# A gated mix of a state-space layer and a GELU MLP: the recurrence as VectorE prefix scans over 256 tokens, GELU as one table function, the first x transposed by TensorE

## The chip, the cores and the metric

The kernel runs on one core of a Trainium2 chip. The metric is the time of one execution on the device in microseconds (us), lower is better. Names of engines as in the profile: PE is TensorE (PEld its weight loads), DVE is VectorE, ACT is ScalarE, POOL is GpSimd, SP is the engine that issues most DMAs.

## What is computed

x has 2048 tokens of 640 features. The state h has 640 complex entries per token; the MLP has 1728 hidden units. All weights are bf16.

```python
g = sigmoid((x * gate_w).sum(-1, keepdims=True))
# a: state-space layer
Lam_bar = exp(dt * Lam)                         # dt = exp(log_dt), Lam complex
Bu = einsum("bld,pd->blp", x, ((Lam_bar - 1.0) / Lam)[:, None] * Bmat)
for t in range(L):
    h = Lam_bar[None, :] * h + Bu[:, t, :]
a = 2.0 * einsum("blp,dp->bld", hseq, Cmat).real + x * Dskip
# b: MLP
b = gelu(x @ w1 + b1) @ w2 + b2                 # tanh form of gelu
out = g * a + (1 - g) * b
```

## The kernel before

**Data.** xT holds x with features on partitions, loaded by transposing DMAs (L334 for the first 512 tokens, L343 for the rest); W1sb, W2sb, BT and CT hold the weights. SP issues all large loads in one fixed order: first half of w1, first x, rest of w1, rest of x, B, w2, C; then, chunk by chunk, x again with tokens on partitions (xtk, L904) and the outputs (L934).

**MLP, in four quarters q of 512 tokens** (`make_mlp`). For each of 14 slices of 128 hidden units (the last has 64) PE runs five 128x512 matmuls into one of two PSUM banks (L651) and ACT copies the bank out with the bias (Ub, L660). Over four slices at a time GELU is computed as u*sigmoid(c*u*(1+0.044715u²)): three DVE passes (L672, L675, L678), a sigmoid on ACT (L686) and a fourth DVE pass into Gl (L693). m2 (L882) then multiplies Gl by W2, 14 matmuls of 128x320 for each half of the output columns.

**State-space layer, in 16 chunks c of 128 tokens** (`make_chunk`). bp (L730) multiplies x by B with tokens on partitions, the gate column beside it; ACT copies it out (L739). DVE multiplies by a complex table that undoes the decay (pre, L763 to L767). PE then sums over the tokens of the chunk by a triangular matrix (L789) and adds the carried state (L791). ACT copies the sums out (L801), DVE computes the next carry (L813 to L817) and multiplies by the complex table of the decay (post, L826 to L830). cp (L852) multiplies by C. ACT scales both branches by the gate (L862, L891) and DVE adds them up (L912, L921, L924).

**Order.** `Sched` is a list scheduler over planned durations; each engine gets its items in one fixed order, the state-space chain at higher priority than the MLP. An engine waits at the head of its queue for semaphores; all items behind it wait too.

Of the kernel before, what the change touches and what calls it, by code (L numbers as in the profile page):

```python
# [13 lines left out]

# [133 lines left out]

def bass_gated_mix__ssm_conv_s5__dense_activation_gelu__prompt_kernel(
# [39 lines left out]
    x2 = A_x[0]

    GC = math.sqrt(0.044715)
    GK = 2.0 * math.sqrt(2.0 / math.pi)
    TWO_PI = 2.0 * math.pi

    with ExitStack() as es, nc.Block() as block:
# [5 lines left out]
        xtk = [SB(f"xtk_{i}", [128, D], BF16) for i in range(2)]  # L201
        xDc = [SB(f"xDc_{i}", [128, D], BF16) for i in range(2)]
        W1sb = SB("W1sb", [128, KD, F], BF16)
        W2sb = SB("W2sb", [128, NF, D], BF16)
        XG = 2
        PADB = 16
        assert (P + PADB) * 2 % 32 == 0 and XG <= PADB
        BT = SB("BT", [128, KD, 2, P + PADB], BF16)
        CT = SB("CT", [128, KP, 2, D], BF16)
        dsk_bc = SB("dsk_bc", [128, D], BF16)  # L210
        b1col = SB("b1col", [128, NF], FP32)
        rows5 = SB("rows5", [KP, 4, 128], BF16)
# [3 lines left out]
        dtf = SB("dtf", [128, KP], FP32)  # L216
        acol = SB("acol", [128, KP], FP32)
        thcol = SB("thcol", [128, KP], FP32)
        io_i = SB("io_i", [128, T + 1], I32)
        io_f = SB("io_f", [128, T + 1], FP32)  # L220
        sg_i = SB("sg_i", [128, T + 1], I32)
        sg_f = SB("sg_f", [128, T + 1], FP32)
        ident = SB("ident", [128, 128], BF16)
        utri = SB("utri", [128, 128], BF16)
        NTB = T + 1
        es_wk = ExitStack()
        es_wk.__enter__()
        WK = [es_wk.enter_context(nc.sbuf_tensor(f"wk{i}", [128, KP, NTB], FP32)) for i in range(7)]
        kq_i = es_wk.enter_context(nc.sbuf_tensor("kq_i", [128, KP, NTB], I32))
        es_wk.__exit__(None, None, None)  # L230
        NES = 6
        Essm = [SB(f"Essm_{i}", [128, D], BF16) for i in range(NES)]
        assert NES * D * 2 <= 8 * KP * NTB * 4
        _pad_wk = SB("pad_wk", [128, (8 * KP * NTB * 4 - NES * D * 2) // 2], BF16)
        ang, tmp1, psi, kq_f, s2t, s4t, magp = WK
        magn = WK[0]
        sint = WK[2]
        cost = WK[3]
        chf = kq_i[:, :, :].bitcast(FP32)
        lr_t, li_t = WK[1], WK[4]  # L240
        nr_t, ni_t = WK[5], WK[6]
        mtmp = [WK[0], WK[2]]
        cwk = SB("cwk", [128, 8, KP], FP32)
        mr_t = SB("mr_t", [128, KP, T], BF16)
        mi_t = SB("mi_t", [128, KP, T], BF16)
        TA = SB("TA", [128, KP, 2, T], BF16)
        TB1 = SB("TB1", [128, KP, 1, T], BF16)
        TBp = TB1[:, :, :, :].broadcast_to([128, KP, 2, T])
        TTa = SB("TTa", [128, KP, 2], BF16)
        TTb = SB("TTb", [128, KP, 2], BF16)  # L250
        MA1 = SB("MA1", [128, 1, P], BF16)
        MA = MA1[:, :, :].broadcast_to([128, 2, P])
        MBp = SB("MBp", [128, 2, P], BF16)
        NU2 = 2
        U2 = [SB(f"U2_{i}", [128, 2, P], BF16) for i in range(NU2)]
        Wt = SB("Wt", [128, 2, P], BF16)
        NUT = 2
        Ut = [SB(f"Ut_{i}", [128, 2, P], BF16) for i in range(NUT)]
        NS2 = 2
        S2 = [SB(f"S2_{i}", [128, KP, 2, T], BF16) for i in range(NS2)]  # L260
        W2t = SB("W2t", [128, KP, 2, T], BF16)
        NH = 2
        Hb = [SB(f"Hb_{i}", [128, KP, 2, T], BF16) for i in range(NH)]
        Rb = SB("Rb", [128, NCH + 1, KP, 2], BF16)
        Rv = SB("Rv", [128, KP, 2], FP32)
        Rw = SB("Rw", [128, KP, 2], FP32)
        gcol = SB("gcol", [128, NCH], FP32)
        g1col = SB("g1col", [128, NCH], FP32)
        NE = 2
        Emlp = [SB(f"Emlp_{i}", [128, D], BF16) for i in range(NE)]  # L270
        osb = [SB(f"osb_{i}", [128, D], BF16) for i in range(2)]
        GROUPS = []
        j = 0
        while j < NF - 1:
            GROUPS.append(list(range(j, min(j + 4, NF - 1))))
            j += 4
        GROUPS.append([NF - 1])
        NGS = 3
        Ub = [SB(f"Ub_{i}", [128, 4, 512], BF16) for i in range(NGS)]
        Qb = [SB(f"Qb_{i}", [128, 4, 512], BF16) for i in range(NGS)]  # L280
        Ib = Qb
        Sgb = Qb
        Gl = [SB(f"Gl_{i}", [128, NF, 512], BF16) for i in range(2)]

        PSB = [es.enter_context(nc.psum_tensor(f"psb{i}", [128, 512], FP32)) for i in range(8)]
        BK_MLP1 = [0, 1]
        BK_ACC = [2, 3]
        BK_U = [4, 5]
        BK_G = [6, 7]

        semnames = [
            "ld_w1a", "ld_w1b", "ld_B", "ld_w2", "ld_C", "ld_misc", "ld_xt0", "ld_xt1", "outdma0", "outdma1",
            "ld_xq0", "ld_xq1",
            "pool", "ld_rows",
            "pe_mlp1", "pe_acc", "pe_u", "pe_g", "pe_misc",
            "act_u", "act_g", "act_e", "act_gate", "act_U", "act_sq", "act_sg", "act_misc",
            "dve_ut", "dve_h", "dve_r", "dve_in", "dve_gl", "dve_o", "dve_misc", "dve_misc2",
        ]
        sems = {n: es.enter_context(nc.semaphore(n)) for n in semnames}
        engines = {"sp": nc.sync, "act": nc.scalar, "dve": nc.vector, "pe": nc.tensor, "pool": nc.gpsimd}  # L300
        E = Emitter(nc, engines, sems)
        sch = Sched()

        def d_act(n):
            return 0.28 + n * 0.00085

        def d_dve(n, mode=1):
            return 0.17 + n * 0.00105 / mode

        def d_mm(n):  # L310
            return max(0.06, n / 2300.0)

        def d_dma(nbytes):
            return 2.0 + nbytes / 150e3

        FH = (NF // 2) * 128

        def f_ld_w1a(eg):
            ins = nc.sync.dma_start(W1sb[:, :, 0:FH], B_w1[:, 0:FH].rearrange("(k p) f -> p k f", p=128))
            return E.inc("sp", ins, "ld_w1a", 16)  # L320

        it_ld_w1a = sch.add("ld_w1a", "sp", 1.0, [], f_ld_w1a, prio=-10, lat=4.0)

        def f_ld_w1b(eg):
            ins = nc.sync.dma_start(W1sb[:, :, FH:F], B_w1[:, FH:F].rearrange("(k p) f -> p k f", p=128))
            return E.inc("sp", ins, "ld_w1b", 16)

        it_ld_w1b = sch.add("ld_w1b", "sp", 1.0, [], f_ld_w1b, prio=-8.9, lat=4.0)
        it_ld_w1 = [it_ld_w1a, it_ld_w1b]

        def f_ld_xq0(eg):
            t = None
            for k in range(KD):
                ins = nc.sync.dma_start_transpose(xT[:, k, 0:512], x2[0:512, k * 128:(k + 1) * 128])  # L334
                t = E.inc("sp", ins, "ld_xq0", 16)
            return t

        it_ld_xq0 = sch.add("ld_xq0", "sp", 1.4 * KD, [], f_ld_xq0, prio=-9, lat=3.0)

        def f_ld_xq1(eg):  # L340
            t = None
            for k in range(KD):
                ins = nc.sync.dma_start_transpose(xT[:, k, 512:S], x2[512:S, k * 128:(k + 1) * 128])  # L343
                t = E.inc("sp", ins, "ld_xq1", 16)
            return t

        it_ld_xq1 = sch.add("ld_xrest", "sp", 2.2 * KD, [], f_ld_xq1, prio=-8.5, lat=6.0)
        it_ld_xq = [it_ld_xq0] + [it_ld_xq1] * (NQ - 1)

        def f_ld_small(eg):  # L350
            E.wait("sp", it_w2pad.done)
            nc.sync.dma_start(W2sb[64:65, NF - 1, :], B_b2.rearrange("(o n) -> o n", o=1)).then_inc(sems["ld_misc"], 16)
            E.count["ld_misc"] += 16
            E.producer.setdefault("ld_misc", "sp")
            ins = nc.sync.dma_start(dsk_bc[:, :], A_Dskip.partition_broadcast(128))
            return E.inc("sp", ins, "ld_misc", 16)

        it_ld_small = sch.add("ld_small", "sp", 1.6, [], f_ld_small, prio=-8, lat=2.0)

        def f_ld_B(eg):  # L360
            t = None
            for k in range(KD):
                for ci, src_ in enumerate((A_B_re, A_B_im)):
                    ins = nc.sync.dma_start_transpose(BT[:, k, ci, 0:P], src_[:, k * 128:(k + 1) * 128])
                    t = E.inc("sp", ins, "ld_B", 16)
            return t

        it_ld_B = sch.add("ld_B", "sp", 1.32 * 2 * KD, [], f_ld_B, prio=-7, lat=6.0)

        def f_ld_w2(eg):  # L370
# [250 lines left out]
        def mark(key, it_):  # L621
            last_use[key] = [it_]
# [391 lines left out]
```

## Time and profile before

| what | value |
|---|---|
| three timed runs | 266.10, 265.36, 266.09 us (median 266.09) |
| span of the profiled execution | 262.7 us |
| median less span | 3.4 us |
| instructions | 4561 |

The span runs from the first to the last instruction of the profiled execution; the time of a run has a few us around it. A group line of the profile reads: line, engine, operation, output<-inputs, shapes, count | busy us, mean ns of one | idle time of the engine just before, and what ended most of it. Matmuls are pipelined, so the mean of one is longer than the step from one to the next; the step is read from a run of many. The other lines are quoted in the prediction where they are used.

### The profile page before, as it was taken

Reading aid. Unit: us, or ns where it says so; the run is one execution under the profiler, and the core shown is the slowest. Engines: PE = TensorE matmul, PEld = TensorE weight load, DVE = VectorE, ACT = ScalarE, POOL = GpSimd, SP = SyncE. Lnnn points to the kernel's source line nnn. Section 1 sums busy time; section 2 is a strip of 40 time slices with the busy share of each in tenths; the row PEclk is TensorE's granted clock in tenths of the full one; section 3 lists DMA queues with packets and bytes.
Section 4 is the critical chain, followed back from the end, with each engine's and each line's share of the span. In section 5 each row is a group of like instructions: output and inputs, shape, how many; then the busy total and the mean of one; then the engine's idle time right before and its main releaser. Section 6 shows DMA issues by size and latency. Waiting matters only on the chain.

```text
span 262.7 us, 4561 instructions
## 1 busy us (share of the span) xinstructions
PE 234.3 (89%) x1863; PEld 161.4 (61%) x1863; DVE 192.5 (73%) x370; ACT 151.1 (58%) x287; POOL 4.0 (2%) x13
## 2 busy tenths in 40 slices
PE   0597608999999999999999999999999998699994
PEld 0232205757767868888889875646777543477773
DVE  3454999687998998869796966897967348972432
ACT  1179906866868747545527626686734277653231
POOL 6000000000000000000000000000000000000000
PEclk9999977999999999999999999999999999999999
DMA  7999689730000000010100010100021100021211
GB/s 214 240 204 179 125 229 260 132 72 25 2 0 0 2 0 2 26 52 2 50 2 1 11 41 2 50 0 2 25 76 52 50 0 2 0 75 51 76 50 50
DMA packets 32037, 16.02 MB, mean 61 GB/s; under 512 B 24785, under 2 KB 32018, under 8 KB 32018
## 3 DMA queue, kind: packets, MB, share of 16 engines
q1 hardware_dynamic: 31826, 15.74, 24.5%
q8 instruction: 14, 0.23, 0.4%
q0 software_dynamic: 192, 0.01, 0.1%
q14 instruction: 5, 0.04, 0.1%
HBM read 7.22 MB, written 2.62 MB: 37 GB/s over the span
## 4 chain that ended last, share of the span: by engine, by line
PE 79%; DVE 9%; ACT 7%; SPq 2%; DMA 1%; issue 1%; DVEq 0%; ACTq 0%
PE psb L882 23%; PE psb L651 17%; PE psb L852 17%; PE psb L730 16%; PE psb L789 3%; PE psb L791 3%; ACT Ub L660 3%; SPq L334 2%; ACT Qb L686 2%; DVE Qb L672 1%; DVE Qb L678 1%; DMA xT<-in_A_x_dram 1%; DVE Qb L675 1%; ACT L484 0%; DVE Gl L693 0%
## 5 line engine op out<-in xcount | busy, mean ns | idle before, releaser
L651 PE MATMUL psb<-xT,W1sb 128*128 128x512 bf16 (+1 forms) x280 | 67.9, 396 | 12.8 <-ACT Ub L660 12.4
L882 PE MATMUL psb<-W2sb,Gl 128*128 128x320 bf16 x448 | 63.2, 299 | 2.2 <-ACT Ub L660 2.2
L651 PEld LDWEIGHTS psb<-xT,W1sb 128*128 128x128 bf16 (+1 forms) x280 | 27.3, 102 | 48.3 <-issue 13.1
L882 PEld LDWEIGHTS psb<-W2sb,Gl 128*128 128x128 bf16 x448 | 43.2, 98 | 20.0 <-ACT Ub L660 3.0
L660 ACT ACTIVATE Ub<-psb,b1col 128x512 bf16<-128x512 f32 (+1 forms) x56 | 37.4, 684 | 25.7 <-PE psb L651 18.8
L730 PE MATMUL psb<-BT,xT 128*128 128x256 bf16 (+2 forms) x480 | 49.4, 255 | 0.1
L852 PE MATMUL psb<-CT,Hb 128*128 128x320 bf16 x320 | 45.8, 299 | 0.0
L730 PEld LDWEIGHTS psb<-BT,xT 128*128 128x128 bf16 x480 | 40.1, 98 | 4.6 <-ACT U_0 L739 0.3
L852 PEld LDWEIGHTS psb<-CT,Hb 128*128 128x128 bf16 x320 | 31.3, 98 | 12.2
L891 ACT ACTIVATE Emlp<-psb,g1col 128x320 bf16<-128x320 f32 x32 | 16.8, 526 | 32.8 <-PE psb L882 32.8
L686 ACT ACTIVATE Qb<-Qb 128x2048 bf16<-128x2048 bf16 (+2 forms) x20 | 27.8, 1397 | 2.3 <-DVE Qb L678 2.2
L672 DVE TENSOR_TENSOR Qb<-Ub 128x2048 bf16<-128x2048 bf16 (+2 forms) x20 | 18.0, 898 | 12.2 <-ACT Ub L660 12.1
L862 ACT ACTIVATE Essm<-psb,gcol 128x320 bf16<-128x320 f32 x32 | 16.1, 528 | 12.6 <-PE psb L852 11.4
L789 PE MATMUL psb<-utri,Ut 128*128 128x128 bf16 x160 | 21.3, 219 | 0.5 <-DVE Ut L767 0.5
L791 PE MATMUL psb<-Rb,ident 128*128 128x128 bf16 x160 | 21.3, 219 | 0.0
L924 DVE TENSOR_TENSOR osb<-osb,Emlp 128x640 bf16<-128x640 bf16 x16 | 7.9, 492 | 17.7 <-ACT Emlp L891 17.4
L693 DVE TENSOR_TENSOR Gl<-Ub,Qb 128x2048 bf16<-128x2048 bf16 (+2 forms) x20 | 17.6, 896 | 3.6 <-ACT Qb L686 3.6
L678 DVE TENSOR_TENSOR Qb<-Qb,Ub 128x2048 bf16<-128x2048 bf16 (+2 forms) x20 | 18.1, 904 | 0.7
L739 ACT CAST U_1<-psb 128x512 bf16<-128x512 f32 (+1 forms) x24 | 12.2, 521 | 10.1 <-PE psb L730 10.1
L789 PEld LDWEIGHTS psb<-utri,Ut 128*128 128x128 bf16 x160 | 15.6, 98 | 1.9 <-DVE Ut L767 0.8
L739 ACT CAST U_0<-psb 128x512 bf16<-128x512 f32 (+1 forms) x24 | 12.3, 516 | 7.3 <-PE psb L730 7.3
L791 PEld LDWEIGHTS psb<-Rb,ident 128*128 128x128 bf16 x160 | 15.7, 98 | 1.1
(113 smaller groups left out, 196.1 us busy)
## 6 DMA issues: line engine op xcount, KB each, us to landing
xtk<-in_A_x_dram SPq DMA_DIRECT2D x16, 160.0 KB, 2.2
out_dram<-osb SPq DMA_DIRECT2D x16, 160.0 KB, 1.8
W2sb<-in_B_w_dram SPq DMA_DIRECT2D x1, 2080.0 KB, 8.6
W1sb<-in_B_w_dram SPq DMA_DIRECT2D x1, 1120.0 KB, 6.0
W1sb<-in_B_w_dram SPq DMA_DIRECT2D x1, 1040.0 KB, 6.0
xT<-in_A_x_dram SPq DMA_TRANSPOSE x10, 5.1
dsk_bc<-in_A_Dskip_dram SPq DMA_DIRECT2D x1, 160.0 KB
BT<-in_A_B_re_dram SPq DMA_TRANSPOSE x5, 3.7
```

Of the source, the lines that this page charges most:

```text
L651: ins = nc.tensor.matmul(PSB[bank][0:rows, :], W1sb[:, k, jf * 128:jf * 128 + rows], xT[:, k, q * 512:(q + 1) * 512], start=(k == 0), stop ...
L660: ins = nc.scalar.activation(Ub[slot][0:rows, jj, :], PSB[bank][0:rows, :], ACT.Identity, bias=b1col[0:rows, jf:jf + 1])
L672: t = E.inc("dve", nc.vector.tensor_tensor(out=Qb[slot][0:rows, 0:ng, :], in0=Ub[slot][0:rows, 0:ng, :], in1=Ub[slot][0:rows, 0:ng, :], op ...
L678: ins = nc.vector.tensor_tensor(out=Ib[slot][0:rows, 0:ng, :], in0=Qb[slot][0:rows, 0:ng, :], in1=Ub[slot][0:rows, 0:ng, :], op=ALU.mult)
L686: ins = nc.scalar.activation(Sgb[slot][0:rows, 0:ng, :], Ib[slot][0:rows, 0:ng, :], ACT.Sigmoid, scale=GK)
L693: ins = nc.vector.tensor_tensor(out=Gl[gsl][0:rows, grp[0]:grp[0] + ng, :], in0=Ub[slot][0:rows, 0:ng, :], in1=Sgb[slot][0:rows, 0:ng, :], ...
L730: t = nc.tensor.matmul(PSB[bank][:, o0:o0 + n_], xT[:, k, c * T:(c + 1) * T], BT[:, k, ci, pb0:pb0 + n_], start=(k == 0), stop=(k == KD - 1))
L739: ins = nc.scalar.copy(U2[u2s][:, :, pb0:pb0 + pw], PSB[bank][:, 0:2 * (pw + xg)].rearrange("p (a w) -> p a w", a=2)[:, :, 0:pw])
L789: nc.tensor.matmul(PSB[bank][:, col0:col0 + T], Ut[uts][:, ci, k * 128:(k + 1) * 128], utri[:, :], start=True, stop=False)
L791: t = nc.tensor.matmul(PSB[bank][:, col0:col0 + T], ident[:, :], Rb[:, c, k, ci:ci + 1].broadcast_to([128, T]), start=False, stop=True)
L852: t = nc.tensor.matmul(PSB[bank][:, 0:HALF], Hb[hs][:, k, ci, :], CT[:, k, ci, hf * HALF:(hf + 1) * HALF], start=(i == 0), stop=(i == 2 * ...
L882: t = nc.tensor.matmul(PSB[bank][:, 0:HALF], Gl[gsl][:, jf, tq * T:(tq + 1) * T], W2sb[:, jf, cols], start=(jf == 0), stop=(jf == NF - 1))
```

## The change

The kernel is written anew around the same mathematics; the two matrix products of the MLP and the product with C keep their shapes.

- **x.** The first 512 tokens arrive with tokens on partitions (`xn`) and PE transposes them in 20 steps (`tp`); DVE and ACT copy them to xT in turn (`tpe`). The other tokens still come by transposing DMA. xn also serves for the gate and the skip term, so the loads of xtk are gone; xn of later quarters is loaded by SP after C. w1 comes in three pieces. The small vectors come through ACT's DMA queue.
- **GELU.** One ACT instruction reads the PSUM bank and writes Gl. The four DVE passes and the sigmoid are gone. m1 has four PSUM banks, shared with the product by B.
- **State-space layer.** The product with B puts the state on partitions (B is the weight, 512 tokens move). For each block of 256 tokens DVE multiplies by a unit rotation (`pre`), runs two real prefix scans h = a*h + v, real and imaginary part (`scan`), rotates the carry, and rotates back (`post`). The sums and the carry on PE, the copies after them, and the chunk tables are gone. The rotation tables are outer products of 16 by 16 angles. A scan covers five state groups of 256 tokens in one instruction; the decay is set to 0 at the start of each group.
- **Gate and output.** The gate sums are DVE instructions with an accumulator (`gates`), its sigmoid is 0.5+0.5*tanh. Two additions on DVE form the output (`cmb`), a third instruction the skip term (`xg`).

```diff
-                            ins = nc.tensor.matmul(PSB[bank][0:rows, :], W1sb[:, k, jf * 128:jf * 128 + rows],
-                        ins = nc.scalar.activation(Ub[slot][0:rows, jj, :], PSB[bank][0:rows, :], ACT.Identity,
-                ins = nc.scalar.activation(Sgb[slot][0:rows, 0:ng, :], Ib[slot][0:rows, 0:ng, :], ACT.Sigmoid, scale=GK)
...
+                    return inc("act", nc.scalar.activation(Gl[q % 2][0:n, jf, :], PS[bank][0:n, :], ACT.Gelu_apprx_tanh, bias=b1col[0:n, jf:jf + 1]))
...
+                    t = nc.tensor.transpose(ps[:, k * 128:(k + 1) * 128], xn[0][:, c, k * 128:(k + 1) * 128], ident[:, :])
...
+            t = inc("dve", nc.vector.tensor_copy(out=atab[:, :, :], in_=amag[:, :].unsqueeze(2).broadcast_to([128, KP, T])))
+            E.wait("dve", t)
+            return inc("dve", nc.vector.memset(atab[:, :, 0:1], 0.0))
...
+        def gates(q):
+                    t = inc("dve", nc.vector.scalar_tensor_tensor(out=scr[:, :], in0=xn[q % 2][:, c, :], scalar=1.0, in1=gwb[:, :],
+                                                                  op0=ALU.mult, op1=ALU.mult, accum_out=gz[:, q * 4 + c:q * 4 + c + 1]))
...
+                            t = nc.tensor.matmul(PS[bank][:, :], BT[:, kd, ci, k * 128:(k + 1) * 128], xT[:, kd, q * 512:(q + 1) * 512],
...
+            def f_pre():
+                t1 = tt(v, bc(mr), u, ALU.mult)
+                t2 = tt(w, bc(mi), u, ALU.mult)
+                E.wait("dve", t1, t2)
+                tt(v[:, 0, :], v[:, 0, :], w[:, 1, :], ALU.add)
+                return tt(v[:, 1, :], v[:, 1, :], w[:, 0, :], ALU.subtract)
...
+                    t = tt(V[:, :, :, 0], V[:, :, :, 0], cz[:, :, :], ALU.add)
+                for ci in range(2):
+                    t = inc("dve", nc.vector.tensor_tensor_scan(out=g[:, ci, :], data0=a, data1=v[:, ci, :], initial=0.0, op0=ALU.mult, op1=ALU.add))
+                if b < NB - 1:
+                    tt(cz[:, :, :], rb(0), ge, ALU.mult)
+                    t = tt(cy[:, 0:2, :], rb(1), ge, ALU.mult)
+                    tt(cz[:, 0, :], cz[:, 0, :], cy[:, 1, :], ALU.add)
+                    t = tt(cz[:, 1, :], cz[:, 1, :], cy[:, 0, :], ALU.subtract)
...
+            def f_cmb():
+                t = tt(osb[c % NO][:, :], xg[c % 2][:, :], E1[c % NE][:, :], ALU.add)
+                E.wait("dve", t)
+                return tt(osb[c % NO][:, :], osb[c % NO][:, :], E2[c % NE][:, :], ALU.add)
...
+        gates(0)
+        m1(0)
+        m1(1)
+        bproj(0)
...
+        for q in range(2, NQ):
+            m1(q)
+            bproj(q)
+            ssm(2 * q)
+            xnload(q, prio=500 * q)
+            gates(q)
+            outs(q - 1)
+            ssm(2 * q + 1)
+        outs(NQ - 1)
```

The orders below list instructions as each engine has them in its queue. First PE at the start of the program, before (rows and b1rows are small vectors, L651 is the first product of the MLP):

```order
L979 UNCONDITIONAL_BRANCH
L439 MATMUL psb<-ident,rows 128x5 x4
L440 MATMUL psb<-ident,b1rows 128x14
L651 MATMUL psb<-xT,W1sb 128x512 x10
L979 UNCONDITIONAL_BRANCH
L651 MATMUL psb<-xT,W1sb 128x512 x10
```

PE at the same place now (xn is x with tokens on partitions, L597 the first product of the MLP):

```order
L808 UNCONDITIONAL_BRANCH
L394 MATMUL ps<-ident,xn 128x128 x5
L415 MATMUL ps<-ident,rows 128x5 x3
L416 MATMUL ps<-ident,b1rows 128x14
L394 MATMUL ps<-ident,xn 128x128 x15
L808 UNCONDITIONAL_BRANCH
L597 MATMUL ps<-xT,W1sb 128x512 x20
```

The transposes of x now stand ahead of the first product, and those of the small vectors among them.

PE in the middle, where the first outputs are made. Before, one chunk's items mix with the next one's (L882 m2, L852 cp, L789 and L791 the sums, L730 bp):

```order
L882 MATMUL psb<-W2sb,Gl 128x320 x14
L979 UNCONDITIONAL_BRANCH
L852 MATMUL psb<-CT,Hb 128x320 x20
L789 MATMUL psb<-utri,Ut 128x128
L791 MATMUL psb<-Rb,ident 128x128
```

PE there now (L618 the product with B of the second quarter, L693 m2, L717 the product with C):

```order
L618 MATMUL ps<-xT,BT 128x512 x20
L693 MATMUL ps<-W2sb,Gl 128x320 x28
L808 UNCONDITIONAL_BRANCH
L693 MATMUL ps<-W2sb,Gl 128x320 x14
L717 MATMUL ps<-CT,H 128x320 x20
L693 MATMUL ps<-W2sb,Gl 128x320 x14
L808 UNCONDITIONAL_BRANCH
L717 MATMUL ps<-CT,H 128x320 x20
L693 MATMUL ps<-W2sb,Gl 128x320 x28
L808 UNCONDITIONAL_BRANCH
L693 MATMUL ps<-W2sb,Gl 128x320 x28
L597 MATMUL ps<-xT,W1sb 128x512 x15
```

The sums are gone from PE, and three halves of m2 stand between the product with B and the first product with C, which needs H of the first block of 256 tokens.

DVE for one chunk of 128 tokens before (carry, post, and pre of a later chunk):

```order
L813 TENSOR_TENSOR Rv<-TTa,S_0 128x10
L814 TENSOR_TENSOR Rw<-TTb,S_0 128x10
L816 TENSOR_TENSOR Rb<-Rv,Rw 128x5
L817 TENSOR_TENSOR Rb<-Rv,Rw 128x5
L826 TENSOR_TENSOR Hb<-TA,S_0 128x1280
L827 TENSOR_TENSOR W2t<-TB,S_0 128x1280
L829 TENSOR_TENSOR Hb<-Hb,W2t 128x5x128
L830 TENSOR_TENSOR Hb<-Hb,W2t 128x5x128
L763 TENSOR_TENSOR Ut<-MA,U_1 128x1280
L764 TENSOR_TENSOR Wt<-MBp,U_1 128x1280
L766 TENSOR_TENSOR Ut<-Ut,Wt 128x640
L767 TENSOR_TENSOR Ut<-Ut,Wt 128x640
```

DVE for one block of 256 tokens now (pre, scan at L658, carry, post; L467 is the line of a helper, c and s are the tables of post):

```order
L467 TENSOR_TENSOR V<-mr,U 128x2560
L467 TENSOR_TENSOR W<-mi,U 128x2560
L467 TENSOR_TENSOR V<-V,W 128x1280 x2
L658 SCALAR_TENSOR_TENSOR G<-atab,V 128x1280 x2
L467 TENSOR_TENSOR cz<-rho,G 128x10
L467 TENSOR_TENSOR cy<-rho,G 128x10
L467 TENSOR_TENSOR cz<-cz,cy 128x5 x2
L467 TENSOR_TENSOR H<-c,G 128x2560
L467 TENSOR_TENSOR W<-s,G 128x2560
L467 TENSOR_TENSOR H<-H,W 128x1280 x2
```

The whole recurrence of a block is now one run on DVE without a step on PE or ACT; the scans stand between pre and post. The tables of functions on ACT are loaded three times in both programs (L457, L484, L686 before; at the first exponential, the first sine and the first GELU now).

More of the change, by code (lines that the diff above doesn't have):

```diff
@@ L261, in bass_gated_mix__ssm_conv_s5__dense_activation_gelu__prompt_kernel @@
[L261 to L266, printed above, removed]
+        amag = SB("amag", [128, KP], FP32)
+        io_i = SB("io_i", [128, 128], I32)
+        io_f = SB("io_f", [128, 128], FP32)
+        st_i = SB("st_i", [128, NS], I32)
+        st_f = SB("st_f", [128, NS], FP32)
+        ident = SB("ident", [128, 128], BF16)
@@ L267, in bass_gated_mix__ssm_conv_s5__dense_activation_gelu__prompt_kernel @@
         gcol = SB("gcol", [128, NCH], FP32)
         g1col = SB("g1col", [128, NCH], FP32)
+        scr = SB("scr", [128, D], BF16)
         NE = 2
[L270 to L279, printed above, removed]
@@ L937, in make_chunk @@
[L937 to L949 removed]
+                    return inc("pe", t)
+                op(f"c_{c}_{hf}", "pe", 2 * KP * d_mm(HALF), [("H", b % NHB), "CT"], [("bank", bank)], f_mm, prio=pe_prio())
@@ new lines, in outs @@
+        def outs(q):
+            for c in range(4 * q, 4 * q + 4):
+                m2(c)
+                cproj(c)
+                comb(c)
+        gates(0)
+        m1(0)
+        m1(1)
+        bproj(0)
+        ssm(0)
+        ssm(1)
+        xnload(1, prio=500)
+        gates(1)
+        bproj(1)
+        ssm(2)
+        outs(0)
+        ssm(3)
+        for q in range(2, NQ):
[6 more added lines that the diff above has]
+            ssm(2 * q + 1)
```

984 lines of the change are left out of this document (389 added, 595 removed).

## The prediction, made before the changed kernel ran

> **What bounds the kernel now.** I read the busy times, the busy slices, the chain and the waits of PE, in this order.
>
> ```profile
> span 262.7 us, 4561 instructions
> PE 234.3 (89%) x1863; PEld 161.4 (61%) x1863; DVE 192.5 (73%) x370; ACT 151.1 (58%) x287; POOL 4.0 (2%) x13
> PE   0597608999999999999999999999999998699994
> DVE  3454999687998998869796966897967348972432
> PE 79%; DVE 9%; ACT 7%; SPq 2%; DMA 1%; issue 1%; DVEq 0%; ACTq 0%
> 66.00:140.00 74.00, 74.00 (x727) 59.38 (x726) 63.91 (x131) 46.79 (x104) 0.00 (x0) 1.00 0.04 13
> PE psb L651 <- ACT Ub L660: 12.4, 6, 7.0
> ```
>
> PE holds 79% of the chain, and from 66 to 140 us it is busy all 74 us, at a granted clock of 1.00. There nothing but fewer or cheaper matmuls gains time. It is idle in the first 10 us, partly so until 44 us (slices of 6.6 us), and at two places near the end. The largest wait of PE, 12.4 us, is for ACT's copies Ub, which in turn wait for the GELU chain on ACT and DVE. DVE is next in line with 192.5 us.
>
> How long PE's work takes without waits I read from long runs in the chain and, for the sums, from the distance of two rows with 16 sums between them (start, us, what):
>
> ```profile
> 9.96 7.17 PE psb L651 x20
> 71.74 1.66 PE psb L730 x20
> 169.53 4.32 PE psb L651 x20
> 190.26 5.43 PE psb L852 x40
> 236.47 22.83 PE psb L882 x168
> ...
> 70.68 0.22 PE L789 MATMUL psb<-utri,Ut 128*128 128x128 bf16 x1
> 71.58 1.82 PE L730 MATMUL psb<-BT,xT 128*128 128x130 bf16 x20
> ```
>
> A step is 4.32/20 = 0.216 us with 512 columns, 22.83/168 = 0.136 with 320 (L852 the same), and 0.90/16 = 0.056 for a sum. So the kernel before holds 280 x 0.216 + 768 x 0.136 + 16 x 2.74 (L730: 1.66 and 1.09 per chunk) + 320 x 0.056 = 60.5 + 104.3 + 43.8 + 17.9 = 226.5 us of PE work; the other 36 us of the span are the start, waits and the tail. The first 20 matmuls took 7.17 instead of 4.32 us: a slow start of 2.85 us.
>
> **What PE does after the change.** The sums go (-17.9). The product with B becomes 200 matmuls of 512 columns, 43.2 us (-0.6). MLP and C stay. PE's work from the first product on is 60.5 + 43.2 + 104.3 = **208.0 us**. If PE never waits, the span is start + slow start + 208 + tail. So three questions are left: when PE starts, whether ACT and DVE keep up, and the tail.
>
> **The start.** Rows of the DMA issues (KB each, us from issue to landing), the column chain, DVE and the tail:
>
> ```profile
> xtk<-in_A_x_dram SPq DMA_DIRECT2D x16, 160.0 KB, 2.2
> W1sb<-in_B_w_dram SPq DMA_DIRECT2D x1, 1040.0 KB, 6.0
> rows<-in_A_Lambda_re_dram POOLq DMA_DIRECT2D x1, 1.2 KB, 5.3
> ...
> 0.74 0.45 SPq L319 DMA_DIRECT2D W1sb<-in_B_w_dram  x1
> 9.33 0.27 PE L439 MATMUL psb<-ident,rows 5*128 5x5 bf16 x4 [9.33 <-DMA b1rows<-in_B_b_dram]
> 10.96 0.83 DVE L469 TENSOR_TENSOR wk<-thcol,sg_f 128x645 f32<-128x645 f32 x1
> ...
> L548 DVE TENSOR_TENSOR wk<-wk,cwk 128x640 f32<-128x640 f32 x1 | 0.8, 827 | 0.0
> L472 DVE TENSOR_SCALAR wk<-wk 128x645 f32<-128x645 f32 x1 | 0.5, 499 | 0.0
> L593 DVE COPY MA<-psb 128x640 bf16<-128x640 bf16 x1 | 0.5, 483 | 0.0
> ```
>
> xn has 640 KB; between 2.2 us at 160 and 6.0 at 1040 KB that is 4.3 us, so it lands at 0.74 + 4.3 = 5.0. Twenty transposes at twice a sum's step (the slow start's ratio or a little more), 2.2 us, and the columns end at about 7.8. But the third copy into xT stands on DVE behind the angle chain: columns at 5.9, plus 1.6 (9.33 to 10.96 before) is 7.5, five operations of 165 elements with their waits 1.6, the decay table of 1280 f32 elements 0.8 to 1.5 (the rates of L472 and L548), the copy 0.5: 10.5 to 11.1. The small loads on ACT's queue have no row: bounds are 2.2 us (SP) and 5.3 us (POOL). The latter puts the columns 2 us later, so the first product starts at 10.5 to 13.1. I take **11.5**, near the SP row since ACT's queue issues like SP's (one more stretch than that, because these loads share the engines with xn). Before it was 9.96: the change loses 1.5 here. The slow start I keep at 2.85; bounds nothing, if the transposes already end it, and 2.85.
>
> The Trainium skill, "TensorE: Matmul & The Clock Gate", Part 1, has the array at half clock until about 3.4 us of activity; the trace's 20 matmuls lost 2.85, which fits a longer stretch of some 5.7 us. By the page's figure the loss is an estimated 1.7 and the sum 1 us less.
>
> **Does ACT keep up?** Rows by form:
>
> ```profile
> L660 ACT ACTIVATE Ub<-psb,b1col 128x512 bf16<-128x512 f32 x52 | 34.7, 684 | 23.5 <-PE psb L651 17.1 <-DVE Gl L693 6.3
> L686 ACT ACTIVATE Qb<-Qb 128x512 bf16<-128x512 bf16 x4 | 2.6, 638 | 0.0
> L891 ACT ACTIVATE Emlp<-psb,g1col 128x320 bf16<-128x320 f32 x32 | 16.8, 526 | 32.8 <-PE psb L882 32.8
> ```
>
> A copy with bias takes 0.68 us, and a table function (sigmoid) of the same size 0.64: no dearer. GELU has no row; between these two it fits into the 5 x 0.216 = 1.08 us in which PE fills the next of four banks, and would up to 1.08. So the 12.4 us of waits go, and ACT is not late next. In the output stage it has four copies of 0.53 in 6.5 us. No table is loaded in the loops, as the change's section says.
>
> **Does DVE keep up?** This is what is late next.
>
> ```profile
> L672 DVE TENSOR_TENSOR Qb<-Ub 128x2048 bf16<-128x2048 bf16 x12 | 14.6, 1221 | 12.2 <-ACT Ub L660 12.1
> L827 DVE TENSOR_TENSOR W2t<-TB,S_1 128x1280 bf16<-128x1280 bf16 x8 | 6.5, 819 | 0.0
> L829 DVE TENSOR_TENSOR Hb<-Hb,W2t 128x640 bf16<-128x640 bf16 x16 | 7.9, 492 | 0.5
> L921 DVE SCALAR_TENSOR_TENSOR osb<-xDc,gcol,Essm 128x640 bf16<-128x640 bf16 x16 | 14.0, 876 | 0.0
> L813 DVE TENSOR_TENSOR Rv<-TTa,S_0 128x10 f32<-128x10 bf16 x8 | 1.4, 173 | 6.4 <-ACT S_0 L801 6.4
> ```
>
> Bf16 products cost 0.52 ns more per element (1221 - 819 over 768), broadcast operand or not (L827 has one): 1.49 us for 2560 elements. Pre is 2 x 1.49 + 2 x 0.82 less overlaps, 4.5 us; post the same; the carry 0.75. A **scan** of 1280 elements has no row. Below, one pass at the f32 rate of L548, 1.5 us; above, two such passes, 3.0, if a step must finish its product before its sum. I take 3.0, since a recurrence waits for its own result and a walk that holds with it holds with less. A block is then 9.75 + 6.0 = 15.75 us. The eight blocks (126), 16 output sums of 0.93, 14 skip terms of 0.8 and the later gates of 7.25 make 159.4 us from the end of bproj(0) on; PE has 166.9 in that time. So DVE fits by 7 us, if it doesn't wait.
>
> The Trainium skill says it plainer, in "DVE: opcode table, instruction layouts, handler registers and perf-mode slots", 6. Datapath and trigger behaviour: the built-in scan runs at half throughput. From the f32 rate that is an estimated 2.8 us; no row here shows it, and the sum would be the same within 1 us.
>
> The walk, from B, the end of bproj(0). PE: bproj(1) to B+10.8, three halves of m2 to 16.5, then it wants H of block 0. DVE: U at 0.7, pre 5.2, scan 11.7, post **16.2**. It holds by 0.3. H1: wanted at 34.7 (with two more products with C, five halves of m2 and three slices of m1), ready at 0.6 past it, as one output sum and two skip terms stand ahead. H2 is wanted at 67, ready at 54; H3 80 and 70; H4, H5 are 30 us early. In bproj(3) ACT's gate tanh waits for gate sums that DVE makes after block 5; the banks fill and PE loses 1.0. H6 is wanted at 146, ready at 134; H7 at 159 and 155. Waits in all **1.6 us**; with a scan of 1.5, none. The tables end at about 38, before B. The gate sums of the second quarter need xn behind C on SP's queue:
>
> ```profile
> 8.51 11.71 SPq L343 DMA_TRANSPOSE xT<-in_A_x_dram  x5
> 21.19 1.14 SPq L364 DMA_TRANSPOSE BT<-in_A_B_re_dram  x1
> 35.85 2.64 SPq L384 DMA_TRANSPOSE CT<-in_A_C_re_dram  x1
> 52.09 1.05 SPq L904 DMA_DIRECT2D xtk<-in_A_x_dram  x2
> ...
> 259.33 0.53 ACT L891 ACTIVATE Emlp<-psb,g1col 128x320 bf16<-128x320 f32 x1 [1.37 <-PE psb L882]
> 259.96 0.49 DVE L924 TENSOR_TENSOR osb<-osb,Emlp 128x640 bf16<-128x640 bf16 x1 [2.51 <-ACT Emlp L891]
> ```
>
> Issues of x took 11.7 us, of B and w2 14.7, of C 16.2; from 2.9 on (four issues of about 0.5) C ends at 45.5, xn lands at 50, the sums end at 53.5, 2 us ahead of pre. Each us later than that would come back as a wait for H0.
>
> **The sum.** Start 11.5, slow start 2.85, 140 matmuls of m1 30.24, bproj(0) 10.8: B = 55.4. Then 32.4 (B) + 30.2 (m1) + 104.3 (outputs) = 166.9, ends at 222.3; waits 1.6; the tail is 3.4 (262.7 less PE's end at 236.47 + 22.83) plus one more sum on DVE, 0.5. Span 227.8. Around the span lie 3.4 us (median 266.09 less 262.7; 2.7 by the lowest run 265.36). **231 us.** Bounds of the terms: start -1.0 to +1.6, slow start -2.85, waits -1.6 to nothing, around -0.7: 225 to 233.
>
> **Rivals.**
> 1. *The start is later* (small loads at 5.3, xn of the second quarter behind busy queues so that H0 slips 1 to 2 us): 233 to 235. For it: POOL's row; against: it's another queue. 0.11.
> 2. *DVE becomes the bound.* From a scan of about 3.4 us on its 159.4 us no longer fit. At 4.4: 55.4 + 0.7 + 111.4 + 16 x 4.4 = 237.9, with 3 of tail and 3.4 around 244. For it: a dependent step per element that no row prices. 0.07.
> 3. *Fixed orders meet the wrong durations* and PE waits for banks again, as it does now for 12.4 us: 243. For it: the planner's figures set the order; against: four banks, and ACT with less than two thirds of PE's time per slice. 0.06.
> 4. *The long bf16 products lose their rate* because the broadcast runs over an outer half: at L548's f32 rate 2560 elements take 2.8 instead of 1.5, four times in eight blocks, 43 us; the change then does what it says and gains nothing, about 265. L827 with its broadcast speaks against it. 0.02.
> 5. *Slower:* the scan costs so much that DVE alone is longer than the whole span before. It decides from 55.4 + 0.7 + 111.4 + 16 S = 259.7, S = 5.8 us, 4.5 ns an element; at 7 us the time is 286. 0.03.
>
> **How the numbers follow.** My forecast, PE bound from the first product on, 225 to 233, has 0.71. Rival 1 adds the stretch to 235, together 0.82; since rivals 2 and 3 have prices on a scale that begins at the forecast, the range goes some way into them: 225 to 240. A measurement of this kernel can tell about 0.3%, 0.8 us. Faster are the forecast and rivals 1 to 3, 0.95; rival 4 splits, 0.01 the same and 0.01 slower, with rival 5 0.04 slower.
>
> **What would show it.** Right: PE's row of slices full from the third slice on, its busy time near 208 plus pipelining, steps of 0.216 and 0.136; no wait of PE for ACT over 1 us; scan rows of 1.5 to 3.0 us; the first L597 at 10.5 to 13; the last slice of PE followed by 4 us. Wrong: PE waiting for H (L717 <- DVE), scans over 3.4 us, products of 2560 elements near 2.8 us, a PE clock below 1.00 in the full stretch.

## The result, and the profile after

| what | before | after |
|---|---|---|
| median of the timed runs | 265.73 us (265.09 to 266.10) | 233.94 us (233.25 to 236.47) |
| ratio | | 0.8819, 95% interval 0.8769 to 0.8870 |
| span of the profiled execution (its time) | 262.7 us | 231.5 us (233.3) |

The change makes the kernel faster by 11.8%. The forecast was 231.0 us, the range 225 to 240. The medians of e2_gate_tanh_late and e7_scan_three in the table further down include one slower run each (238.17 and 250.29 us), which their ratios leave out. The page of the profile after, in the rows that were shown of before:

```profile
span 231.5 us, 3235 instructions
PE 213.0 (92%) x1261; PEld 123.6 (53%) x1272; DVE 189.4 (82%) x263; ACT 102.1 (44%) x173; POOL 2.5 (1%) x11
PE   1499999997599899999999999999999999999993
DVE  2899997003899999999999999999996999999411
PE 57%; SPq 21%; DVE 16%; DMA 2%; issue 1%; ACT 1%
...
L658 DVE TENSOR_TENSOR_SCAN G<-atab,V 128x1280 bf16<-128x1280 f32 x16 | 44.3, 2811 | 0.3
L604 ACT ACTIVATE Gl<-ps,b1col 128x512 bf16<-128x512 f32 (+1 forms) x56 | 38.5, 687 | 23.9 <-PE ps L597 23.9
L467 DVE TENSOR_TENSOR V<-mr,U 128x2560 bf16<-128x2560 bf16 x8 | 11.9, 1490 | 3.1 <-ACT U L627 2.9
```

PE is full from the third slice to the last, but for one hole, the slices with 7 and 5 (52 to 64 us). DVE has zeros just ahead of it. The chain says the same: before, PE held 79% of it; now SP's issues and DVE hold 37%, nearly all of that ahead of 95 us. The waits of PE after the change:

```profile
PE ps L394 <- DMA xn<-in_A_x_dram: 5.1, 1, 5.1
PE ps L618 <- ACT U L627: 3.9, 1, 3.9
PE ps L597 <- DVE xT L403: 2.7, 1, 2.7
PE ps L717 <- DVE H L467: 1.6, 2, 1.1
```

The first and the third are the start. The second is the hole: PE waits for a copy of U on ACT, an engine that is busy 44% of the time. What held ACT is read from the timeline, of which these are some rows (start, us, what, idle before it and what ended it):

```profile
3.01 16.15 SPq L336 DMA_TRANSPOSE xT<-in_A_x_dram  x5
11.24 14.04 PE L597 MATMUL ps<-xT,W1sb 128*128 128x512 bf16 x57 [2.65 <-DVE xT L403]
43.25 13.12 PE L618 MATMUL ps<-xT,BT 128*128 128x512 bf16 x59
51.23 0.58 SPq L329 DMA_DIRECT2D xn<-in_A_x_dram  x1
55.97 0.82 DVE L571 SCALAR_TENSOR_TENSOR scr<-xn,gwb 128x640 bf16<-128x640 bf16 x1 [16.82 <-DMA xn<-in_A_x_dram]
59.43 0.20 ACT L578 ACTIVATE gth<-gz 128x4 f32<-128x4 f32 x1 [6.74 <-DVE scr L571]
60.27 4.04 PE L618 MATMUL ps<-xT,BT 128*128 128x512 bf16 x18 [3.89 <-ACT U L627]
75.85 2.89 PE L717 MATMUL ps<-CT,H 128*128 128x320 bf16 x20 [1.07 <-DVE H L467]
94.72 5.61 PE L717 MATMUL ps<-CT,H 128*128 128x320 bf16 x40 [0.49 <-DVE H L467]
```

Read upwards: PE's bank is freed by a copy that stands on ACT behind the gate tanh (L578); that waits 6.74 us for the gate sums (L571) on DVE; those wait 16.82 us for xn of the second quarter, which SP issues only at 51.23, because its queue holds the transposing loads of x, B and C ahead of it. DVE had nothing to do all that time. Pre of block 0 began at 60.64; by the prediction's walk it was to begin 0.7 us after the first product with B, which ends at 54.05. The last two rows are what came of it for DVE: PE waits 1.07 us for H of block 0 and 0.49 for H of block 1.

### The profile page after: what moved, and what is told of

The parts are those of the page before. It is cut to its first block, busy times and chain, and to the rows that moved or that the text cites. A ratio compares the mean times of both kernels' runs of the same rounds, so it can differ in the third digit from the quotient of the medians.

```text
span 231.5 us, 3235 instructions
## 1 busy us (share of the span) xinstructions
PE 213.0 (92%) x1261; PEld 123.6 (53%) x1272; DVE 189.4 (82%) x263; ACT 102.1 (44%) x173; POOL 2.5 (1%) x11
## 4 chain that ended last, share of the span: by engine, by line
PE 57%; SPq 21%; DVE 16%; DMA 2%; issue 1%; ACT 1%
PE ps L693 20%; SPq L336 20%; PE ps L717 17%; PE ps L597 12%; PE ps L618 9%; DVE G L658 5%; DVE V L467 3%; DVE H L467 3%; DVE W L467 2%; DMA xn<-in_A_x_dram 2%; SPq L329 2%; DVE scr L571 1%; DVE osb L467 1%; DVE xg L733 1%; ACT U L627 0%
## 5 line engine op out<-in xcount | busy, mean ns | idle before, releaser
L597 PE MATMUL ps<-xT,W1sb 128*128 128x512 bf16 (+1 forms) x273 | 62.2, 385 | 3.0 <-DVE xT L403 2.7
L693 PE MATMUL ps<-W2sb,Gl 128*128 128x320 bf16 x448 | 63.4, 299 | 0.0
L693 PEld LDWEIGHTS ps<-W2sb,Gl 128*128 128x128 bf16 x448 | 43.8, 98 | 17.6
L604 ACT ACTIVATE Gl<-ps,b1col 128x512 bf16<-128x512 f32 (+1 forms) x56 | 38.5, 687 | 23.9 <-PE ps L597 23.9
L717 PE MATMUL ps<-CT,H 128*128 128x320 bf16 x320 | 45.9, 299 | 1.6 <-DVE H L467 1.6
L618 PE MATMUL ps<-xT,BT 128*128 128x512 bf16 x196 | 43.5, 379 | 4.2 <-ACT U L627 3.9
L597 PEld LDWEIGHTS ps<-xT,W1sb 128*128 128x128 bf16 (+1 forms) x280 | 27.4, 100 | 37.1 <-issue 3.9
L658 DVE TENSOR_TENSOR_SCAN G<-atab,V 128x1280 bf16<-128x1280 f32 x16 | 44.3, 2811 | 0.3
L717 PEld LDWEIGHTS ps<-CT,H 128*128 128x128 bf16 x320 | 31.1, 98 | 14.5 <-DVE H L467 2.4
L618 PEld LDWEIGHTS ps<-xT,BT 128*128 128x128 bf16 x200 | 19.2, 97 | 28.3 <-issue 5.6
L627 ACT ACTIVATE U<-ps 128x512 bf16<-128x512 f32 x40 | 23.3, 595 | 14.9 <-PE ps L618 14.9
L571 DVE SCALAR_TENSOR_TENSOR scr<-xn,gwb 128x640 bf16<-128x640 bf16 x16 | 13.2, 823 | 17.3 <-DMA xn<-in_A_x_dram 16.8
L467 DVE TENSOR_TENSOR V<-mr,U 128x2560 bf16<-128x2560 bf16 x8 | 11.9, 1490 | 3.1 <-ACT U L627 2.9
L467 DVE TENSOR_TENSOR V<-V,W 128x1280 bf16<-128x1280 bf16 x16 | 12.5, 821 | 0.3
L467 DVE TENSOR_TENSOR H<-H,W 128x1280 bf16<-128x1280 bf16 x16 | 12.5, 820 | 0.3
L467 DVE TENSOR_TENSOR H<-c,G 128x2560 bf16<-128x2560 bf16 x8 | 11.9, 1487 | 0.1
L467 DVE TENSOR_TENSOR W<-s,G 128x2560 bf16<-128x2560 bf16 x8 | 11.9, 1484 | 0.0
## 6 DMA issues: line engine op xcount, KB each, us to landing
W1sb<-in_B_w_dram SPq DMA_DIRECT2D x1, 1040.0 KB, 10.6
```

The costliest lines, as they stand in the source:

```text
L467: return inc("dve", nc.vector.tensor_tensor(out=o, in0=a, in1=b, op=o_))
L597: t = nc.tensor.matmul(PS[bank][0:n, :], W1sb[:, k, jf * 128:jf * 128 + n], xT[:, k, q * 512:(q + 1) * 512], start=(k == 0), stop=(k == KD ...
L604: return inc("act", nc.scalar.activation(Gl[q % 2][0:n, jf, :], PS[bank][0:n, :], ACT.Gelu_apprx_tanh, bias=b1col[0:n, jf:jf + 1]))
L618: t = nc.tensor.matmul(PS[bank][:, :], BT[:, kd, ci, k * 128:(k + 1) * 128], xT[:, kd, q * 512:(q + 1) * 512], start=(kd == 0), stop=(kd = ...
L627: return inc("act", nc.scalar.activation(dst, src, ACT.Copy, scale=1.0 if ci == 0 else -1.0))
L658: t = inc("dve", nc.vector.tensor_tensor_scan(out=g[:, ci, :], data0=a, data1=v[:, ci, :], initial=0.0, op0=ALU.mult, op1=ALU.add))
```

## The experiments

Six of them (e1, e2, e4, e5, e9, e10) only move items of the finished order, each within its engine, so that the other items keep theirs: `move(engine, item, other)` puts an item ahead of another. The other four (e3, e6, e7, e8) change instructions. xn1 is the load of x of the second quarter, gth1 its gate tanh, tpe2 the third copy into xT, psi the angle chain, cols the transposes of the small vectors, dt the exponential of the rates, w2a and w2b the loads of w2. The kernel before ran beside each; ratios are to it. Span and granted clock are of the profiled execution.

| kernel | median us | ratio, 95% interval | span | granted clock |
|---|---|---|---|---|
| the change | 233.94 | 0.8819, 0.8769 to 0.8870 | 231.5 | 1.000 |
| e1_xn_early | 228.11 | 0.8597, 0.8562 to 0.8632 | 226.0 | 1.000 |
| e2_gate_tanh_late | 235.40 | 0.8844, 0.8803 to 0.8885 | 234.2 | 0.985 |
| e3_gelu_alone | 254.87 | 0.9599, 0.9580 to 0.9618 | 252.5 | 0.986 |
| e4_third_copy_first | 235.76 | 0.8858, 0.8820 to 0.8895 | 234.4 | 0.978 |
| e5_both | 226.43 | 0.8524, 0.8503 to 0.8544 | 224.3 | 1.000 |
| e6_sums_back | 244.67 | 0.9229, 0.9187 to 0.9270 | 242.6 | 1.000 |
| e7_scan_three | 247.18 | 0.9288, 0.9246 to 0.9330 | 245.6 | 0.969 |
| e8_x_by_dma | 228.39 | 0.8601, 0.8586 to 0.8617 | 226.2 | 1.000 |
| e9_w2_behind_xn | 229.98 | 0.8655, 0.8634 to 0.8676 | 228.2 | 0.997 |
| e10_start | 225.47 | 0.8505, 0.8459 to 0.8551 | 223.9 | 1.000 |

The intervals of e2 and e4 overlap that of the change: by their times they can't be told from it, and what they show is where the waits stand.

### Is it the load of xn? e1_xn_early

```diff
+        move('sp', 'xn1', 'B')
```

> Only the load of xn for the second quarter is moved, ahead of the loads of B on SP's queue. Theory A (the late xn holds both ACT, by the gate tanh, and DVE, by the gate sums ahead of the first block): all waits of PE after its first product go, 3.9 + 1.1 + 0.5 = 5.5 us, so the span falls from 231.5 to about 226.0. Theory B (PE waits in the second product with B because ACT's copies of U are too slow or the banks too few): the 3.9 us stay, the span falls by 1.6 at most, to 229.9 or more.

The span is 226.0, and PE has no wait left after its first product. The late load alone cost 5.5 us of span, all the later waits of the change (3.9 + 1.6).

### Or the place of the gate tanh? e2_gate_tanh_late

```diff
+        move('act', 'gth1', 'e1_0_0')
+        move('dve', 'g1', 'pre1')
```

> The load stays late. On ACT the gate tanh of the second quarter moves behind all ten copies of U of that quarter, and on DVE the two small instructions that use it move behind the first block. Theory A: ACT no longer stops, PE's 3.9 us in the product with B go, but the first block on DVE still waits for the gate sums that wait for xn, so H of block 0 comes at about 74.7 instead of 75.8 and PE waits there for some 3.8 us instead: span 230.3, about 1.2 less. Theory B': only the blocked ACT costs time: span 227.6.

A wait of PE (us in total, times, longest), and two pieces of the chain:

```profile
PE ps L717 <- DVE H L467: 4.4, 1, 4.4
```

```profile
76.73 5.41 PE ps L717 x20
84.04 2.72 PE ps L717 x20
```

The wait for U is gone, and the wait for H has taken its place, as expected: DVE still makes the gate sums ahead of pre. The span is 3.9 longer than expected. The first 20 products behind the wait took 5.41 us, the next 20 2.72: 2.7 us more, some 0.2 of it for filling the pipeline again (the 40 products behind the change's wait for H of block 1 took 5.61 instead of 5.43) and 2.5 by a lower clock (below). The load itself was issued at 53.42 here, 2.2 later than in the change, and H of block 0 came at 76.73 instead of 74.7; against that, the 0.5 us that the change waits for H of block 1 is gone. Together that is 4.0 us.

### How the load came to be late: e9_w2_behind_xn

The five issues of the rest of x before, by their line (shortest, median and longest in ns), and the first of them in the chain of the change:

```profile
L343 SPq DMA_TRANSPOSE xT<-in_A_x_dram x5: 1338/2109/3257, 8.5 to 18.2; - x5
```

```profile
3.01 7.99 SPq L336
```

The first one now takes 7.99 us, where before none took over 3.26. In the same profile the first three of C, behind the loads of w2, take 2.41, 2.90 and 1.86, the others 1.27.

The order of w2 was then moved in the changed kernel:

```diff
+        move('sp', 'w2a', 'xn1')
+        move('sp', 'w2b', 'xn1')
+        move('sp', 'xn1', 'w2a')
```

> The changed kernel with one step moved on SP's queue: the two loads of w2 (2160 KB) stand behind the x of the second quarter instead of ahead of C. Theory A (a transposing issue takes 1.27 us by itself, and longer only while large loads ahead of it are still in the queue): the first three issues of C, 2.41, 2.90 and 1.86 us with w2 ahead, fall to about 1.3 each, so that x of the second quarter is issued at 46.0 instead of 51.23 (1.8 for the issue of w2, 3.4 for C), lands at 50.7, TensorE waits neither for U nor for H, and the span is 226.0. Theory B (each issue has its own length, the first ones of C are long): x is issued only 1.8 us earlier, at 49.4, TensorE still waits 2.1 us for U, and the span is 229 to 230.

SP's timeline, and a wait of PE:

```profile
2.94 17.64 SPq L336 DMA_TRANSPOSE xT<-in_A_x_dram  x5
28.51 2.46 SPq L336 DMA_TRANSPOSE BT<-in_A_B_re_dram  x1
34.96 1.28 SPq L336 DMA_TRANSPOSE CT<-in_A_C_re_dram  x1
36.28 1.27 SPq L336 DMA_TRANSPOSE CT<-in_A_C_im_dram  x1
37.59 1.27 SPq L336 DMA_TRANSPOSE CT<-in_A_C_re_dram  x1
48.10 0.58 SPq L329 DMA_DIRECT2D xn<-in_A_x_dram  x1
```

```profile
PE ps L717 <- DVE H L467: 1.6, 2, 1.1
```

Theory A holds for the issues of C: every one takes 1.27 or 1.28 once w2 no longer stands ahead. That an issue is longer only behind large loads does not hold: one of B took 2.46, with no plain load on SP's queue for 25 us before it. Nor does every large load ahead make it long: in the kernel before the five of the first x, right behind 1040 KB of w1, took 1.21 to 1.39 each. The load came at 48.10, 3.1 us earlier, not 5.2, since the issues of x took 1.5 more here than in the change's profile, and those of B 0.6 more. PE no longer waits for U; 1.6 us for H stay, and the span is 228.2. That is near the prediction's 227.8, with the same 1.6 us of waits, but by luck: the prediction had 0.6 for H of block 1, 1.0 for U in the last product with B and nothing for block 0, while here block 0 waits 1.08, block 1 0.50, and the last product with B not at all. All of the 1.6 still hangs on the load, since with an early one (e1) no wait is left.

### The start: e4_third_copy_first, e5_both, e8_x_by_dma, e10_start

```diff
+        move('dve', 'tpe2', 'psi')
```

> On DVE the third copy of transposed x moves ahead of the angle chain and the decay table; nothing else. The first product then starts at about 9.4 instead of 11.24. Theory A: with xn of the second quarter as late as before, everything gained at the start is lost again in the wait for it: span 231.5, no change. Theory B: the waits are not tied to the load, the whole row of work moves up: 229.7.

The wait, and the load and the products behind it in the chain:

```profile
PE ps L618 <- ACT U L627: 7.8, 1, 7.8
```

```profile
54.02 4.38 DMA xn<-in_A_x_dram
62.72 7.91 PE ps L618 x25
```

The first product came 1.8 earlier, at 9.40, the second product with B 1.5 earlier, and all of it went into the wait, as expected. xn was issued 2.8 later than in the change's profile (the first issue of x took 9.72 us), so that PE went on at 62.72 instead of 60.27, and the 25 products behind the wait took 7.91 instead of 25 x 0.216 = 5.4. Against these 5.0 us stand the 1.6 us of waits for H, which this kernel no longer has; that leaves 3.4, where the span passes the expected by 2.9. Nothing ties the later load to the moved copy: SP's order is that of the change, and the first issue of x took between 7.99 and 9.72 us in the nine kernels with this order ahead of it, the change at the low end.

With both moves:

> e1 and e4 together. Theory A: 231.5 - 5.5 - 1.8 = 224.2 us span, PE without a wait from its first product on unless DVE now becomes late: DVE's row from the first block on has little idle time, so a wait for H of 0 to 2 us may come back. Theory B: 228 or more.

224.3, as expected; the first product starts at 9.60, and nothing waits after it. A gain at the start counts only once the late load is gone.

```diff
-                    t = nc.tensor.transpose(ps[:, k * 128:(k + 1) * 128], xn[0][:, c, k * 128:(k + 1) * 128], ident[:, :])
...
+        move('sp', 'xn1', 'B')
+        move('sp', 'xn0', 'w1_1')
+            for k in range(KD):
+                dma_inc("sp", nc.sync.dma_start_transpose(xT[:, k, 0:512], x2[0:512, k * 128:(k + 1) * 128]), "l_xT0")
```

> e1_xn_early with the first 512 tokens of x brought in by five transposing DMAs again, right behind the first piece of w1, and the 20 transposes on PE and their copies left out; xn follows for the gate. The five take about 6.6 us of SP's queue, so all later loads are issued that much later. Theory A (the transposes on PE pay by freeing SP's queue, not by the start): first product at 10.0 to 10.8 instead of 11.24, but waits of 2 to 5 us for w1, the rest of x or B: span 227 to 230 (e1_xn_early 226.0). Theory B (the loads have room): 224.8 to 225.3.

226.2, in neither theory's span; PE waits 4.9 us for xT. This is the 226.0 of e1 again: transposing the first x on PE gains nothing while the third copy stands behind the angle chain. With that copy moved (e5) it is 1.9 ahead. Behind xn and two pieces of w1 the first issue of the rest of x took 5.50 us here.

```diff
+        move('pe', 'cols', 'm1_0_0')
+        move('act', 'tpe1', 'dt')
+        move('act', 'tpe3', 'dt')
-        move('dve', 'tpe2', 'psi')
+        move('dve', 'tpe2', 'cols1')
```

> On e5_both, TensorE makes all 20 transposes of the first x before it touches the columns, ScalarE copies its two tiles before it scales the rates, VectorE makes the third copy before the second columns copy. Theory A: the first product stood behind the columns and their load (9.60 us in e5_both), not behind the transposes; the first product starts at about 8.1 us, no later wait appears, the span is 222.8 us (224.3 - 1.5). Theory B: something else that the first products or the first GELU need (the weights, the rest of x, the table load behind the later columns) is late in its place, PE waits once more between 10 and 26 us, and the span stays within 0.5 us of 224.3.

The first piece of the MLP in the chain of e5_both, then of e10_start:

```profile
9.60 7.16 PE ps L597 x25
```

```profile
8.33 7.98 PE ps L597 x25
```

The product starts 1.27 earlier and nothing new waits, but the first 25 take 0.82 longer. That the earlier start is the reason isn't shown: this loss also differs between kernels that start alike (below). The span gains 0.4; the intervals of e5 and e10 overlap, so the two can't be told apart. They are the fastest kernels here.

### What each part is worth: e3_gelu_alone, e6_sums_back, e7_scan_three

e3 is the kernel before with GELU as one function, and the gate by tanh; the scheduler then ordered its items anew:

```diff
...
-                        ins = nc.scalar.activation(Ub[slot][0:rows, jj, :], PSB[bank][0:rows, :], ACT.Identity,
+                        ins = nc.scalar.activation(Gl[gsl][0:rows, jf, :], PSB[bank][0:rows, :], ACT.Gelu_apprx_tanh,
...
```

> The kernel before with one part of the change alone: GELU as one table function from PSUM into Gl (the gate by tanh, so that no table is reloaded in the loops; six table loads at the start instead of three). Theory A (the change gains from two sources of like size, the waits that the GELU chain puts on PE and the sums that leave PE): PE's work 226.5 + start 10.0 + slow start 2.9 + tail 3.4 = 242.8 us if no wait is left, with 0 to 7 us of waits at the start for ACT's tables and two banks: span 243 to 250. Theory B (GELU's passes lay beside PE's work anyway, nearly all of the gain is the sums): 257 or more.

The median falls by 4.0%, some 10.6 us, a smaller gain than theory A had and a larger one than B: the span of 252.5 lies in neither range. In its profile 5.9 of the 12.4 us in which PE waited for ACT are left. Its ACT loads function tables six times at the start (1.28 us each), three of them among the first copies of GELU; if the waits come from that, which no run separates, GELU by itself is worth more than the 10.6.

e6 is e5 with as many matmuls of 128 columns as the sums had:

```diff
+                    for k in range(2 * KP):
+                        nc.tensor.matmul(PS[bank][:, 0:128], ident[:, :], xT[:, k % KD, 0:128], start=True, stop=True)
...
```

> e5_both plus 320 matmuls of 128 columns on PE, ten ahead of each product with C, whose results are overwritten: PE does the work of the sums again. Theory A (PE bound throughout): 320 x 0.056 = 17.9 us more, span 242.2. Theory B (PE waits for DVE's H in the output stages, so matmuls there are partly free): less than 8 more, below 232.

18.3 us: the sums cost their own time (17.9 by the prediction) where PE sets the end. e7 is e5 with the scan of the imaginary part made twice, each scan waiting for the one ahead of it:

```diff
-                for ci in range(2):
+                for ci in (0, 1, 1):
+                    if t is not None:
+                        E.wait("dve", t)
```

> e5_both with a third scan in each block of 256 tokens (the second one done twice, same result), 2.8 us more on DVE per block, 22.5 in all. In e5_both H of block 1 is ready when PE wants it, H of block 7 5.0 us ahead. Theory A (DVE is just behind PE): the first two blocks bring 5.5 us of waits at once, in all 12 to 18 more, span 236 to 243. Theory B (DVE has room): less than 5 more.

Its waits of PE, and the granted clock in 40 slices:

```profile
PE ps L618 <- ACT U L627: 9.7, 1, 9.7
PE ps L719 <- DVE H L467: 5.6, 3, 2.6
```

```profile
PEclk9999999999997999999999999999858999999998
```

Of 22.5 us more on DVE 21.3 reach the span, more than either theory gave. The waits behind the first product sum to 15.9, as theory A had it: DVE has little to spare behind PE. The longest stands in the last product with B, where the copies of U wait behind the gate tanh for gate sums that DVE now makes too late. Most of the rest is slower products: about 1.7 behind the wait for H of block 0, 1.8 behind that of 9.7 us, and 1.3 more at the start than in e5.

## Why the prediction was right, and where its sum was off

| term | predicted | measured |
|---|---|---|
| first product (L597) | 11.5 | 11.24 |
| slow start | 2.85 | 1.77 |
| 140 matmuls of m1 and bproj(0) | 41.04 | 41.04 |
| PE's work after that | 166.9 | 168.2 |
| waits | 1.6 | 5.45 |
| tail | 3.9 | 3.8 |
| span | 227.8 | 231.5 |
| around the span | 3.4 | 1.8 |

Measured: m1 runs from 11.24 to 43.25, 32.01 us for 30.24 of work. bproj(0) ends at 43.25 + 10.8 = 54.05, PE's last product at 227.69; less the waits of 3.89, 1.07 and 0.49 that is 168.2.

The median of 233.94 lies in the range, but 0.9 above the 233 that the forecast's own terms allowed: it is in the stretch to 235 that rival 1 added, with a chance of 0.11. Two of the prediction's signs came out on the wrong side: a wait of PE for ACT of 3.9 us (at most 1 was the sign of right), and waits for H of 1.6.

**Right:** that PE sets the end, with steps of 0.216 and 0.136, full after the hole; that ACT keeps up with GELU (687 ns, between the sigmoid's 638 and what PE leaves); that a product of 2560 elements keeps its bf16 rate (1490 ns, rival 4 falls); that DVE nearly fits (its waits go with the late load), with a scan of 2811 ns for the 3.0 taken (rivals 2 and 5 fall; they began at 3.4 and 5.8). The start came by the way it was worked out: xn landed in 4.3 us, and the third copy behind the angle chain was the last to release PE. The half rate for the scan that the Trainium skill states in "DVE: opcode table, instruction layouts, handler registers and perf-mode slots", 6. Datapath and trigger behaviour, agrees: 2.8 was estimated from it, 2.81 measured.

**The mis-sized step** is the cover of the second quarter's gate sums: "C ends at 45.5, xn lands at 50, the sums end at 53.5, 2 us ahead of pre". C ended at 51.18, xn landed at 55.94, the sums ended at 59.4, and the waits were 5.45 instead of 1.6. The working moved SP's queue forward by the 5.6 us that the rest of x is issued earlier and kept each issue's duration from before. But that duration was no property of the issue: the five of x took 16.15 instead of 11.71, 4.4 of the 5.7 us by which C ended late, since the first was held 7.99 us behind xn and the three pieces of w1, where none was held so before. So C ended at 51.2 after the change and at 52.0 before, though the rest of x was issued 5.5 us earlier. That issues are held by loads ahead of them is shown by e9 for C, and argued from the rows for x: held 7.99 to 9.72 us in the nine kernels with this order, 5.50 in e8, and no more than 3.26 before. What makes one load hold an issue and another not stays open. The prediction named the late load in rival 1 and gave it 1 to 2 us by way of H of block 0. That way cost 1.6, and 3.9 came by one that it had seen only for the last quarter: the tanh of the gate on ACT holds the copies of U behind it (e2). The 1.0 us that it had for the last quarter did not come. With the load early all 5.5 us go (e1), so the sum's 1.6 was not the right figure either.

**Smaller:** the slow start was 1.1 less than the 2.85 of before. The estimate of 1.7 from the Trainium skill, "TensorE: Matmul & The Clock Gate", Part 1, was nearer here; e10's first 25 products lost 2.6, so that it is no constant. Nor does the moment of the start set it: counted as in the table (m1's time less 30.24), e2 lost 3.2 with the start of the change, and e7 3.3 with that of e5, which lost 2.0. The granted clock reads 1.00 all this while, so its row does not show the slow start. The time around the span is 1.8 in every run of the new kernel; the 3.4 set a median of other runs against one profiled span. These two, and the start's -0.3, against +3.9 of waits and +1.3 of PE's work (whose cause is open), leave the profiled run 2.3 over the forecast, and the median 2.9.

**Where the 32 us came from.** GELU alone gives some 10.6 on the kernel before, the sums 18.3 on the new one. Their sum of 29 is no exact split, since each was measured beside another rest, but it leaves little for the rest: the start lost 1.3, the slow start gave 1.1 back. With the load and the third copy in their places (e5) the gain is 39 us.

## What to carry to other kernels

The time that a transposing load held its queue was no constant here, and it changed with the loads ahead of it (2.90 us and 1.27 for the same load in e9's comparison), so the moment at which a later load comes is not found by adding issue durations of another order; where a small load feeds a chain, give it a place ahead of large ones. Look for the waits in the queue behind an instruction, too: a 0.2 us tanh on an engine that is half idle stopped PE for 3.9 us. A gain ahead of such a wait (e4) is worth nothing until the wait is gone.

## What was not expected of the hardware

After some waits of PE the granted clock fell for some microseconds. The granted clock in 40 slices, of e4_third_copy_first (5.9 us each):

```profile
PEclk9999999998579999999999999999999999999999
```

and of e2_gate_tanh_late:

```profile
PEclk9999999999999599999999999999999999999999
```

The low digits begin within these waits, of 7.8 and 4.4 us, and the products behind them took 2.5 and 2.7 us longer than their steps, some 0.2 of it for filling the pipeline. The kernel before has it too, around its longest wait of 7.0 us: 0.50 from about 36 to 42.7 us. Shorter waits can do it: in e3 the clock fell to 0.50 behind a wait of 3.3, and in e7 behind one of 2.4, that for H of block 0. There it was low from about 73.4 to 76.8, and the 20 products, 2.72 us at full rate, took 4.58:

```profile
72.91 4.58 PE ps L719 x20
```

In the four kernels without such a wait (e1, e5, e6, e10) the clock was 1.00 in every run; e8's was at least 0.997. The change itself, with its wait of 3.9, was granted 1.00 in two of four runs (span 231.5 in both) and 0.985 in two (232.8 and 234.7); that the same mechanism is behind the latter is argued, since no trace of them was taken. The Trainium skill, "TensorE: Matmul & The Clock Gate", Part 1, has the array fall back to half clock after an idle window of about 3.4 us, with windows that run free of the program. The change's four runs fit that: a wait of 3.9 us holds a whole window in some runs and not in others. e7's wait of 2.4 us does not, since it is shorter than the window; in that run less than a whole idle window was enough. Where the clock fell, it cost some 1.7 to 2.5 us beyond the wait in e2, e4 and e7; in the change's profile it did not fall, and the wait of 3.9 cost no more than itself.

The accumulator of a gate sum is a second instruction on DVE, DVE_READ_ACCUMULATOR, of 0.08 us.
